# Block-causal attention feeding a max-of-two MLP on one core: a new order of the opening loads, and batch 1's transposes moved to a later step

## The chip, the core and the metric

The kernel runs on one core of a Trainium2 chip. The core has five engines that run their own instruction streams: TensorE (PE, with its weight loads as PEld), VectorE (DVE), ScalarE (ACT), GpSimd (POOL) and SyncE (SP). Each stream is executed in its own order; semaphores hold an instruction back until what it needs is there. Transfers issued by SP, ACT and POOL run on the same 16 DMA engines. The metric is the time of one execution in microseconds (us).

## What is computed

Eight batches, eight heads, 576 positions of 64 numbers; the MLP has 4608 tokens, 512 model columns and 1024 hidden ones.

```python
scores = scale * np.matmul(q, k.transpose(0, 1, 3, 2))
mask = (pos[:, None] // 64) >= (pos[None, :] // 64)
scores = np.where(mask, scores, -1e9)
attn = np.exp(scores - np.max(scores, axis=-1, keepdims=True))
attn = attn / (np.sum(attn, axis=-1, keepdims=True) + 1e-09)
attn_out = np.matmul(attn, v)                       # (8, 8, 576, 64)
x = attn_out.transpose(0, 2, 1, 3).reshape(8 * 576, 512)
g = np.maximum(x @ w1, x @ w2)
out = g @ w_out
```

## The kernel before

The attention is cut into 32 pairs of heads (`NPAIR`), four to a batch (`HP`); two pairs are a group g (16 groups, two to a batch). The loop at the end of the kernel takes one pair at each step s, 0 to 31. The streams of all engines stand in the order in which this loop writes them: nothing is reordered afterwards.

A step s has these parts. `burst_a`, called A(s) below, multiplies q and k for the first half of the score blocks into two tiles u0 and u1 of the PSUM pool `ps_s` (two buffers); ACT takes the exponential (line 258) into the tile `aT`, and POOL clears the masked corners (line 263). `burst_b`, B(s), does the rest in u2 and u3; u2 takes the buffer of u0 and u3 that of u1, so PE waits there for ACT. Between A and B stand the transposes (line 235) of one half (q or k) of the next group, T below; they need the bf16 copy of that half (`cast`, line 105, on POOL in most steps), which needs its load (`load_qk`, line 95, issued by SP into one of two raw buffers). Where `gated` is set, a tiny POOL memset into the raw buffer makes the load wait for POOL's place in the order. `copy_out` (line 242) takes the transposed q or k out of PSUM. Then `av(p, ...)` multiplies the weights of a pair by V (line 303) in two halves, avXa and avXb for pair X, and DVE normalises (lines 309, 310). `PLAN` says which pairs' av a step does: none in steps 0 and 1, pair 0 in step 2, pairs 1, 2 and 3 in step 3, none in 4 and 5, and pair s-2 from step 6 on. `x_out(g)` transposes a group's result into xT (lines 323 to 329); after the last group of a batch its 576 tokens are ready for the MLP.

The MLP is a long list of matmuls of 512 columns, called fills: units h (line 165, x by w1, then x by w2, eight matmuls to each 128 hidden columns; DVE copies the first product and takes the maximum, lines 172 and 174) and y (line 183, g by w_out; ACT copies, line 189, SP stores). `fill(n)` writes the next n of them where it stands, as far as their tokens are ready. The first 64 are the units h of the first 512 tokens, h0.0 to h0.7, and the next 32 its units y, y0.0 to y0.3. All fills, T, x_out and av take tiles of one PSUM pool, `ps_m`, with four buffers. `fill_of(s)` sets how many fills a step gets.

POOL issues the loads that change type (to bf16): V (`load_v`, line 109, five chunks c0 to c4 for a batch), w1 and w2 (`load_w`, line 120) and w_out (`load_wo`, line 123). Before the change the loads of batch 1's V stand in steps 3, 4 and 5 (`v_loads`), and those of w_out in step 5, ahead of the last chunk of V.

Of the kernel before, what the change touches and what calls it, by code (L numbers as in the profile page):

```python
# [14 lines left out]
def kernel(  # L15
# [73 lines left out]
    def load_qk(g, queues, gated=False):  # L89
        b, u = divmod(g, GPB)  # L90
        for nm, src, queue in (("q", q, queues[0]), ("k", k, queues[1])):
            raws[nm, g] = t = raw.tile([P, 2, RPP * D], FP32, name=f"{nm}raw")
            if gated:
                nc.gpsimd.memset(t[:, 0, :1], 0.0)
            queue.dma_start(
                out=t[:],
                in_=src[b, 4 * u:4 * u + 4].rearrange(
                    "(s h) (p t) d -> (h p) s (t d)", h=2, t=RPP),
            )

    def cast(nm, g, parts):
        t = raws.pop((nm, g)).rearrange("p s (t d) -> p t s d", d=D)
        qk_n[nm, g] = n = qkn.tile([P, RPP, 2, D], BF16, name=f"{nm}n")
        for copy, j0, j1 in parts:
            copy(out=n[:, j0:j1], in_=t[:, j0:j1])  # L105

    def load_v(b, c):
        rows = min(P, S - c * P)
        nc.gpsimd.dma_start(  # L109
            out=vv_r[b % NV][:rows, c, :, :D],  # L110
            in_=v[b, :, c * P:c * P + rows, :].rearrange("h p d -> p h d"),
        )
# [5 lines left out]
    def load_w(f0, fw):  # L118
        for dst, src in ((w1_sb, w1r), (w2_sb, w2r)):
            nc.gpsimd.dma_start(out=dst[:, :, f0:f0 + fw], in_=src[:, :, f0:f0 + fw])  # L120

    def load_wo(c0, n):
        nc.gpsimd.dma_start(out=wo_sb[:, c0:c0 + n, :], in_=wor[:, c0:c0 + n, :])
# [97 lines left out]
    def fill(n):  # L221
        for _ in range(min(n, ready())):
            next(moe_steps)
            at[0] += 1
# [4 lines left out]
    def transposes(nm, g, copies):  # L229
        n = qk_n.pop((nm, g))  # L230
        pts = [ps_m.tile([P, RPP, NP], BF16, name=f"ps_{nm}T", tag="m") for _ in range(2)]
        for j in range(RPP):
            for i in range(2):
                r = slice(i * NP, (i + 1) * NP)
                nc.tensor.transpose(  # L235
                    pts[i][:, j, :], n[r, j].rearrange("p s d -> p (s d)"), ident[r, r],
                )

        def copy_out():
            for i in range(2):  # L240
                t = (qT_r if nm == "q" else kT_r)[(2 * g + i) % NT]
                copies[i](  # L242
                    out=t[:, :S].rearrange("q (p j) -> q p j", j=RPP),
                    in_=pts[i].rearrange("q j p -> q p j"),
                )
        return copy_out
# [18 lines left out]
    def burst_a(p):  # L265
        u0 = ps_s.tile([P, 2, 512], FP32, name="ps_s", tag="s")
        scores(p, u0, 0, 0, 0, 512)
        u1 = ps_s.tile([P, 2, 512], FP32, name="ps_s", tag="s")
        scores(p, u1, 0, 0, 512, 64)
        scores(p, u1, 64, 1, 128, 448)  # L270
        exp(p, u0, 512, 0)
        mask(p, 0)
        exp(p, u1, 512, 512)
        mask(p, 576)

    def burst_b(p):
        u2 = ps_s.tile([P, 2, 512], FP32, name="ps_s", tag="s")
        scores(p, u2, 0, 2, 256, 320)
        scores(p, u2, 320, 3, 384, 192)
        u3 = ps_s.tile([P, 2, 512], FP32, name="ps_s", tag="s")  # L280
        scores(p, u3, 0, 4, 512, 64)
        exp(p, u2, 512, 1024)
        mask(p, 1024)
        mask(p, 1344)
        exp(p, u3, 64, 1536, m=BLK)
# [29 lines left out]
    def x_out(g):  # L315
        b, u = divmod(g, GPB)
        xp = xps.pop(g)
        pe = ps_m.tile([P, 2, NCH, BLK], BF16, name="ps_xe", tag="m")
        po = ps_m.tile([P, 2, NCH - 1, BLK], BF16, name="ps_xo", tag="m")
        for s in range(2):  # L320
            for t in range(NCH):
                src = xp[:, t, s].rearrange("p a d -> p (a d)")
                nc.tensor.transpose(pe[:, s, t, :], src[:BLK], ident[:BLK, :BLK])  # L323
                if t < NCH - 1:
                    nc.tensor.transpose(po[:, s, t, :], src[BLK:], ident[BLK:, BLK:])
        dst = xT[:, 2 * u:2 * u + 2, b * S:b * S + NCH * P].rearrange(
            "p s (t h w) -> p s t h w", h=2, w=BLK)
        nc.vector.tensor_copy(out=dst[:, :, :, 0], in_=pe[:])
        nc.vector.tensor_copy(out=dst[:, :, :NCH - 1, 1], in_=po[:])  # L329
        if u == GPB - 1:  # L330
            done_tokens[0] = (b + 1) * S
# [6 lines left out]
    def fill_of(s):  # L338
        if s >= NPAIR - LAG:
            return 27  # L340
        left = 10 - s if s < 10 else 4 - (s - 2) % 4
        return -(-ready() // left)

    def v_loads(s):
        at_ = {3: [(1, 0), (1, 1)], 4: [(1, 2), (1, 3)], 5: [(1, 4)]}
        if s in at_:
            todo = at_[s]
        else:
            nb, i = divmod(s + 2, HP)
            todo = [(nb, c) for c in ((0, 1), (2, 3), (4,), ())[i]] if s > 5 and nb < B else []  # L350
        for nb, c in todo:
            load_v(nb, c)

    cq = transposes("q", 0, (dve, act))
    ck = transposes("k", 0, (act, dve))
# [3 lines left out]
    for s in range(NPAIR):  # L359
        g, i = divmod(s, 2)  # L360
        avs = PLAN.get(s, [s - LAG])
        n = fill_of(s)
        if x_due and s > HP:
            x_out(x_due.pop())
        burst_a(s)
        if x_due and s == HP:
            x_out(x_due.pop())
            n = fill_of(s)
        if s == 0:
            cast("k", 1, ((dve, 0, RPP),))  # L370
        fill(n * 2 // 5)
        copy_out = None
        if g + 1 < NG:
            copy_out = transposes("qk"[i], g + 1, (dve, dve if s < HP else act))
            if s < HP:
                copy_out()
        burst_b(s)
        if copy_out and s >= HP:
            copy_out()
        if i == 0 and g + 2 < NG:  # L380
            load_qk(g + 2, (SP, SP), gated=s < HP)
        if g + 2 - (i == 0) < NG and s > 0:
            cast("kq"[i], g + 1 + i, ((pool, 0, RPP),))
        if s == 0:
            load_w(512, 512)
        if s == 5:
            load_wo(0, 4)
            load_wo(4, 4)
        v_loads(s)
        for p in avs:  # L390
            av(p, [0, 1])
            if s >= HP:
                fill(n // 5)
            av(p, [2, 3, 4])
            if p % 2:
                x_due.append(p // 2)
            if p == 2:
                x_out(x_due.pop())
        fill(n - n * 2 // 5 - n // 5 * (len(avs) > 0 and s >= HP))
    for p in range(NPAIR - LAG, NPAIR):  # L400
        if x_due:
            x_out(x_due.pop())
# [3 lines left out]
        fill(11)  # L406
    x_out(NG - 1)
    fill(len(needs))


# [28 lines left out]
```

## Time and profile before

| what | us |
|---|---|
| median of 3 runs | 317.12 (317.08 to 317.22) |
| the profiled execution's own time | 318.27 |
| its span in the profile | 316.5 |
| PE busy | 276.1 (87%) |
| DVE, ACT, POOL busy | 180.3, 135.9, 97.0 |
| PE idle that ended with V's load | 9.6 |
| PE idle at T that ended with a cast of q on POOL | 9.4 |

Rows of the timeline give start, duration, engine, line, operation and tiles, count, and in brackets the idle time before with what ended it. A row of several matmuls lasts until the last one's end, so the next row of the engine can start before it ends. Rows of groups end with the idle time of the engine and its releasers. Rows of waits give total, times and longest.

### The profile page before, as it was taken

To read this page: it belongs to the slowest core of one execution; us is meant where nothing else is said; L and a number is where in the kernel's file an instruction comes from. 1 tells how busy PE (TensorE), PEld (TensorE's weight loads), DVE (VectorE), ACT (ScalarE), POOL (GpSimd) and SP (SyncE) were. 2 spreads that over 40 slices of the span, in tenths; PEclk is the share of its full clock that TensorE was granted. 3 is DMA by queue.
4 is the path that set the end of the run, shared out by engine and by line. 5 is a ranking of instruction groups with operands and counts; after the bars stand their busy time and mean duration, and the time that the engine had idled before them with its cause. 6 is when DMAs were issued, how large, how long until landed. Compare 5 with 4: busy or idle time off the path is not lost.

```text
span 316.5 us, 7360 instructions
## 1 busy us (share of the span) xinstructions
PE 276.1 (87%) x3072; PEld 142.7 (45%) x3072; DVE 180.3 (57%) x361; ACT 135.9 (43%) x195; POOL 97.0 (31%) x217
## 2 busy tenths in 40 slices
PE   1517894399899999999999999999999999999995
PEld 1305542144554554455445554555454554444442
DVE  5504873163587856575667566756675675646440
ACT  3634373047755573447344734373534401010112
POOL 3934476043283263325331533153300000000000
PEclk9999999589999999999999999999999999999999
DMA  7999989908498157628672867286300000101113
GB/s 280 106 240 238 330 114 177 148 0 100 114 310 146 35 35 100 194 76 143 89 206 64 156 79 214 53 166 70 74 35 33 35 35 33 69 35 64 50 52 133
DMA packets 55649, 36.65 MB, mean 116 GB/s; under 512 B 38720, under 2 KB 42816, under 8 KB 55616
## 3 DMA queue, kind: packets, MB, share of 16 engines
q0 software_dynamic: 41728, 7.87, 30.6%
q1 hardware_dynamic: 13616, 27.73, 25.3%
q8 instruction: 24, 0.39, 0.5%
q10 hardware_dynamic: 272, 0.59, 0.5%
q14 instruction: 9, 0.07, 0.1%
HBM read 34.60 MB, written 9.44 MB: 139 GB/s over the span
## 4 chain that ended last, share of the span: by engine, by line
PE 75%; DMA 8%; POOL 6%; issue 4%; DVE 3%; ACT 3%; ACTq 0%; POOLq 0%; DVEq 0%
PE ps_h L165 37%; PE ps_y L183 19%; PE ps_o L303 9%; PE ps_s L252 6%; DMA qraw<-in_q_dram 4%; DMA vv<-in_v_dram 4%; ACT aT L258 3%; PE ps_kT L235 2%; POOL vv L109 1%; PE ps_xe L323 1%; POOL qn L105 1%; DVE kT L242 1%; DVE xp L310 1%; PE ps_qT L235 1%; POOL kn L105 1%
## 5 line engine op out<-in xcount | busy, mean ns | idle before, releaser
L165 PE MATMUL ps_h<-xT,w_sb 128*128 128x512 bf16 x576 | 138.5, 382 | 0.6 <-DVE xT L329 0.4
L258 ACT ACTIVATE aT<-ps_s 128x1024 bf16<-128x1024 f32 (+1 forms) x128 | 98.9, 833 | 90.4 <-PE ps_s L252 88.8
L165 PEld LDWEIGHTS <-w_sb 128*128 128x128 bf16 x576 | 53.4, 98 | 62.1 <-issue 6.8
L172 DVE CAST h<-ps_h 128x512 bf16<-128x512 f32 x72 | 49.6, 689 | 53.3 <-PE ps_h L165 53.3
L183 PE MATMUL ps_y<-wo_sb,g 128*128 128x512 bf16 x288 | 70.1, 379 | 0.0
L263 POOL MEMSET aT<- 64x128 bf16 x128 | 23.2, 199 | 139.3 <-ACT aT L258 138.9
L189 ACT COPY y<-ps_y 128x512 f32<-128x512 f32 x36 | 21.1, 586 | 82.1 <-PE ps_y L183 57.3
L174 DVE TENSOR_TENSOR g<-h,ps_h 128x512 bf16<-128x512 bf16 x72 | 49.4, 686 | 9.6 <-PE ps_h L165 7.9
L303 PE MATMUL ps_o<-vv,aT 128*128 128x65 bf16 x960 | 39.6, 196 | 10.6 <-DMA vv<-in_v_dram 9.6
L252 PE MATMUL ps_s<-qT,kT 64*128 64x64 bf16 (+4 forms) x384 | 37.9, 295 | 8.8 <-ACT aT L258 8.1
L303 PEld LDWEIGHTS <-aT 128*128 128x128 bf16 x960 | 34.5, 99 | 20.5 <-issue 9.9
L183 PEld LDWEIGHTS <-g 128*128 128x128 bf16 x288 | 26.6, 98 | 30.0 <-issue 1.3
L109 POOL DMA_DIRECT2D vv<-in_v_dram x40 | 33.7, 848 | 0.0
L310 DVE TENSOR_TENSOR xp<-ps_o,rec 128x256 bf16<-128x256 f32 x64 | 31.4, 491 | 2.2
L309 DVE RECIPROCAL rec<-ps_o 128x4 f32<-128x4 f32 x64 | 11.9, 186 | 33.3 <-PE ps_o L303 32.8
L252 PEld LDWEIGHTS <-kT 64*128 64x128 bf16 x384 | 18.0, 98 | 22.5 <-issue 16.6
L235 PE MATMUL ps_qT<-ident,qn 64*128 64x64 bf16 x288 | 8.1, 199 | 15.8 <-POOL qn L105 9.4
L105 POOL CAST qn<-qraw 128x1152 bf16<-128x1152 f32 (+1 forms) x16 | 18.1, 1133 | 11.2 <-DMA qraw<-in_q_dram 10.3
L242 DVE COPY qT<-ps_qT 128x576 bf16<-128x576 bf16 x18 | 13.4, 752 | 13.7 <-PE ps_qT L235 13.4
L242 DVE COPY kT<-ps_kT 128x576 bf16<-128x576 bf16 x18 | 13.4, 753 | 8.4 <-PE ps_kT L235 8.2
L105 POOL CAST kn<-kraw 128x1152 bf16<-128x1152 f32 (+1 forms) x15 | 16.6, 1103 | 0.8
L235 PEld LDWEIGHTS <-qn 64*128 64x128 bf16 x288 | 6.3, 100 | 21.2 <-POOL qn L105 10.3
(31 smaller groups left out, 84.7 us busy)
## 6 DMA issues: line engine op xcount, KB each, us to landing
qraw<-in_q_dram SPq DMA_DIRECT2D x16, 576.0 KB, 4.5
out_dram<-y SPq DMA_DIRECT2D x36, 256.0 KB, 2.0
kraw<-in_k_dram SPq DMA_DIRECT2D x15, 576.0 KB, 5.3
vv<-in_v_dram POOLq DMA_DIRECT2D x32, 128.0 KB, 4.2
w_sb<-in_moe_w_dram POOLq DMA_DIRECT2D x4, 256.0 KB, 7.5
w_sb<-in_moe_w_dram POOLq DMA_DIRECT2D x2, 512.0 KB, 12.7
wo_sb<-in_moe_w_out_dram POOLq DMA_DIRECT2D x2, 512.0 KB, 8.8
kraw<-in_k_dram ACTq DMA_DIRECT2D x1, 576.0 KB, 5.4
```

The costliest lines, as they stand in the source:

```text
L105: copy(out=n[:, j0:j1], in_=t[:, j0:j1])
L109: nc.gpsimd.dma_start(out=vv_r[b % NV][:rows, c, :, :D], in_=v[b, :, c * P:c * P + rows, :].rearrange("h p d -> p h d"),)
L165: nc.tensor.matmul(pt[:], w_sb[:, c, f * P:(f + 1) * P], xT[:, c, t0:t0 + SPAN], start=(c == 0), stop=(c == NDM - 1),)
L172: nc.vector.tensor_copy(out=h1[:], in_=pt[:])
L174: nc.vector.tensor_max(g[:, f, :], h1[:], pt[:])
L183: nc.tensor.matmul(py[:], g[:, f, s * P:(s + 1) * P], wo_sb[:, f, :], start=(f == 0), stop=(f == NFF - 1),)
L235: nc.tensor.transpose(pts[i][:, j, :], n[r, j].rearrange("p s d -> p (s d)"), ident[r, r],)
L242: copies[i](out=t[:, :S].rearrange("q (p j) -> q p j", j=RPP), in_=pts[i].rearrange("q j p -> q p j"),)
L252: nc.tensor.matmul(ps[:m, hh, col:col + w], kT[r, c * P:c * P + m], qT[r, q0:q0 + w], start=True, stop=True,)
L258: nc.scalar.activation(out=aT_r[p % NA][:m, :, a0:a0 + w], in_=ps[:m, :, :w], func=AF.Exp, scale=scale,)
L303: nc.tensor.matmul(po[:, gi, hh, :], a[:, hh, a0:a0 + P], vv[:, c, h0 + 2 * hh, :], start=(mm == 0), stop=(mm == n_mm - 1),)
L310: nc.vector.tensor_mul(xp[:, ts[0]:ts[0] + n, :, p % 2], po[:, :, :, :D], rec[:, :n].to_broadcast([P, n, 2, D]),)
```

## The change

The loads of the opening get a new order on POOL and SP, written out step by step in `pool_work`: q and k of group 3 move from step 2 to step 1 (behind the gates of group 2 in step 0); V of batch 1 moves ahead of the casts of groups 2 and 3, to steps 2, 3 and 4; w_out stands in step 5 behind all of it. The cast of q of group 2 moves from POOL in step 1 to ACT in step 3, that of k from POOL in step 2 to POOL in step 3, and the casts of group 3 from steps 3 and 4 to step 4. The loads of group 4 stay in step 4. The transposes of group 2 move out of steps 2 and 3 to the beginning of step 4, between two lots of 6 fills; those of group 3 stand together in step 5. In step 4 x_out(1) and these 12 fills come before A(4). A step's fills are dealt out otherwise: half of them (before, two fifths) between A and T in steps with more than 12, and a sixth (before, a fifth) between the two halves of av.

```diff
-    def v_loads(s):
-        at_ = {3: [(1, 0), (1, 1)], 4: [(1, 2), (1, 3)], 5: [(1, 4)]}
-        if s in at_:
-            todo = at_[s]
+    def pool_work(s):
+        g, i = divmod(s, 2)
+        if s == 0:
+            load_qk(2, (SP, SP), gated=True)
+            load_w(512, 512)
+        elif s == 1:
+            load_qk(3, (SP, SP), gated=True)
+        elif s == 2:
+            load_v(1, 0)
+            load_v(1, 1)
+        elif s == 3:
+            load_v(1, 2)
+            cast("q", 2, ((act, 0, RPP),))
+            cast("k", 2, ((pool, 0, RPP),))
+        elif s == 4:
+            load_v(1, 3)
+            load_v(1, 4)
+            cast("q", 3, ((pool, 0, RPP),))
+            cast("k", 3, ((pool, 0, RPP),))
+            load_qk(4, (SP, SP))
+        elif s == 5:
+            load_wo(0, 4)
+            load_wo(4, 4)
+            cast("q", 4, ((pool, 0, RPP),))
         else:
-            nb, i = divmod(s + 2, HP)
-            todo = [(nb, c) for c in ((0, 1), (2, 3), (4,), ())[i]] if s > 5 and nb < B else []
-        for nb, c in todo:
-            load_v(nb, c)
+            if i == 0 and g + 2 < NG:
+                load_qk(g + 2, (SP, SP))
+            if g + 1 + i < NG:
+                cast("kq"[i], g + 1 + i, ((pool, 0, RPP),))
+            nb, j = divmod(s + 2, HP)
+            if nb < B:
+                for c in ((0, 1), (2, 3), (4,), ())[j]:
+                    load_v(nb, c)
+
+    T_AT = {s: [("qk"[s % 2], s // 2 + 1)] for s in range(NPAIR - 2)}
+    T_AT[2] = T_AT[3] = T_AT[4] = []
+    T_AT[5] = [("q", 3), ("k", 3)]
+
+    def t_pair(s):
+        outs = [transposes(nm, g, (dve, dve if s < HP else act)) for nm, g in T_AT.get(s, [])]
+        return lambda: [f() for f in outs]
...
-        if x_due and s > HP:
+        if x_due:
             x_out(x_due.pop())
+        if s == HP:
+            n = fill_of(s)
+            fill(6)
+            cq = transposes("q", 2, (dve, act))
+            ck = transposes("k", 2, (dve, act))
+            cq()
+            ck()
+            fill(6)
         burst_a(s)
-        if x_due and s == HP:
-            x_out(x_due.pop())
-            n = fill_of(s)
         if s == 0:
             cast("k", 1, ((dve, 0, RPP),))
-        fill(n * 2 // 5)
-        copy_out = None
-        if g + 1 < NG:
-            copy_out = transposes("qk"[i], g + 1, (dve, dve if s < HP else act))
-            if s < HP:
-                copy_out()
-        burst_b(s)
-        if copy_out and s >= HP:
+        n_a = n // 2 if n > 12 else n * 2 // 5
+        n_b = n // 6 if avs and s >= HP else 0
+        fill(n_a)
+        if s < HP:
+            t_pair(s)()
+            burst_b(s)
+        else:
+            copy_out = t_pair(s)
+            burst_b(s)
             copy_out()
-        if i == 0 and g + 2 < NG:
-            load_qk(g + 2, (SP, SP), gated=s < HP)
-        if g + 2 - (i == 0) < NG and s > 0:
-            cast("kq"[i], g + 1 + i, ((pool, 0, RPP),))
-        if s == 0:
-            load_w(512, 512)
-        if s == 5:
-            load_wo(0, 4)
-            load_wo(4, 4)
-        v_loads(s)
+        pool_work(s)
         for p in avs:
             av(p, [0, 1])
-            if s >= HP:
-                fill(n // 5)
+            fill(n_b)
...
-        fill(n - n * 2 // 5 - n // 5 * (len(avs) > 0 and s >= HP))
+        fill(n - n_a - n_b)
```

Three places of the new order, each with the line of before marked - and that of after marked +. POOL first, in steps 1 to 3; `vv_99` is V of batch 1, `aT_102` to `aT_104` are cleared in steps 1 to 3, and the first `CAST qn` is q of group 2.

```order
 L120 DMA w_sb<-in_moe_w_dram 128x4x512 x2
 L263 MEMSET aT_102 64x2x64 x4
-L105 CAST qn<-qraw 128x1152
-L263 MEMSET aT_103 64x2x64 x4
 L94 MEMSET qraw 128x1
 L94 MEMSET kraw 128x1
+L263 MEMSET aT_103 64x2x64 x4
+L109 DMA vv_99<-in_v_dram 128x8x64 x2
+L263 MEMSET aT_104 64x2x64 x4
+L109 DMA vv_99<-in_v_dram 128x8x64
```

The cast that stood ahead of the gates of group 3 is gone from POOL, and three chunks of batch 1's V stand where group 3's casts were waited for. Next, POOL in steps 4 and 5, where the last chunks of that V and w_out are issued:

```order
+L109 DMA vv_99<-in_v_dram 128x8x64
+L109 DMA vv_99<-in_v_dram 64x8x64
 L105 CAST qn<-qraw 128x1152
-L109 DMA vv_99<-in_v_dram 128x8x64 x2
-L263 MEMSET aT_101 64x2x64 x4
 L105 CAST kn<-kraw 128x1152
-L109 DMA vv_99<-in_v_dram 128x8x64 x2
 L263 MEMSET aT_102 64x2x64 x4
+L123 DMA wo_sb<-in_moe_w_out_dram 128x4x512 x2
 L105 CAST qn<-qraw 128x1152
-L123 DMA wo_sb<-in_moe_w_out_dram 128x4x512 x2
-L109 DMA vv_99<-in_v_dram 64x8x64
```

The last chunk of V stood behind w_out and now stands ahead of it, with two casts of group 3 between. Last, PE of the changed kernel at the beginning of step 4, with the semaphores that each waits for (`ps_h_573` is the second product of h0.0, of which two matmuls are left; `DVE` and `Activation` stand for copies out of PSUM):

```order
L165 MATMUL ps_h_573<-xT_105,w2_sb_107 128x512 [waits PE_49]
...
L235 LDWEIGHTS qn_402 [waits Activation_49]
L235 MATMUL ps_qT_576<-ident_109,qn_402 128x64 [waits PE_49]
...
L235 LDWEIGHTS kn_404 [waits Pool_49]
L235 MATMUL ps_kT_596<-ident_109,kn_404 128x64 [waits DVE_49]
L235 LDWEIGHTS kn_404
L235 MATMUL ps_kT_597<-ident_109,kn_404 128x64 [waits Activation_49]
```

The transposes of k of group 2 follow those of q directly, and their second tile waits for ACT's copy of q's second tile, since the half-done product holds one of the four buffers.

## The prediction, with its working

> **What bounds the kernel now.** I read the page's slices first, then PE's groups, its waits, the chain of work and the transfers.
>
> ```profile
> PE   1517894399899999999999999999999999999995
> PEclk9999999589999999999999999999999999999999
> L303 PE MATMUL ps_o<-vv,aT 128*128 128x65 bf16 x960 | 39.6, 196 | 10.6 <-DMA vv<-in_v_dram 9.6
> L235 PE MATMUL ps_qT<-ident,qn 64*128 64x64 bf16 x288 | 8.1, 199 | 15.8 <-POOL qn L105 9.4
> ```
>
> A slice is 7.9 us. PE is full from the ninth slice on; what is missing lies in the first five and in the seventh and eighth, and in the eighth the granted clock falls to 0.5. The next rows are of the windows of a whole batch in the middle, and of PE's waits from 64 us to the end:
>
> ```profile
> 142.10:173.97 31.87, 30.75 (x372) 16.24 (x372) 20.03 (x41) 16.60 (x26) 11.50 (x25) 1.00 0.62 127
> PE ps_s L252 <- ACT aT L258: 5.5, 10, 0.7
> PE ps_o L303 <- DVE xp L310: 0.3, 2, 0.2
> ```
>
> PE is busy for 30.75 of 31.87 us there, and its waits after 64 us come to 5.8 us. So PE bounds everything behind the opening, and the time changes by what the opening moves. The chain of work shows the opening's two great waits, and the transfers issued in two short windows show their sizes (last number: us from issue to landing):
>
> ```profile
> 16.35 7.94 DMA qraw<-in_q_dram
> 24.44 1.15 POOL qn L105
> 48.37 12.16 DMA vv<-in_v_dram
> ...
> wo_sb<-in_moe_w_out_dram POOLq DMA_DIRECT2D x1, 512.0 KB, 10.3
> vv<-in_v_dram POOLq DMA_DIRECT2D x1, 64.0 KB, 12.2
> ...
> w_sb<-in_moe_w_dram POOLq DMA_DIRECT2D x2, 512.0 KB, 12.7
> kraw<-in_k_dram SPq DMA_DIRECT2D x1, 576.0 KB, 10.4
> ```
>
> First, T of q of group 2 stands in step 2 and waits for a load that lands at 24.3. Second, av4 in step 6 waits for the last 64 KB of batch 1's V, which were issued behind w_out and took 12.2 us.
>
> **The change part by part.** No matmul, cast, copy or byte is added or removed, so the steps are placed again on PE's line with these rows of the timeline:
>
> ```profile
> 13.29 1.04 PE L252 MATMUL ps_s<-qT,kT 64*128 64x512 bf16 x6 [1.06 <-ACT aT L258]
> 15.93 0.23 PE L252 MATMUL ps_s<-qT,kT 64*128 64x64 bf16 x2 [0.30 <-ACT aT L258]
> 16.84 1.04 PE L252 MATMUL ps_s<-qT,kT 64*128 64x512 bf16 x6 [0.68 <-ACT aT L258]
> 25.64 0.66 PE L235 MATMUL ps_qT<-ident,qn 64*128 64x64 bf16 x18 [7.76 <-POOL qn L105]
> 26.71 1.83 PE L303 MATMUL ps_o<-vv,aT 128*128 128x65 bf16 x30
> 31.25 2.00 PE L303 MATMUL ps_o<-vv,aT 128*128 128x65 bf16 x60
> 31.73 0.17 DVE L309 RECIPROCAL rec<-ps_o 128x4 f32<-128x4 f32 x1
> 37.29 0.41 DVE L329 COPY xT<-ps_xo 128x512 bf16<-128x512 bf16 x1
> 37.76 1.02 PE L165 MATMUL ps_h<-xT,w_sb 128*128 128x512 bf16 x4 [0.38 <-DVE xT L329]
> 38.99 0.41 PE L252 MATMUL ps_s<-qT,kT 64*128 64x320 bf16 x6
> 39.34 2.33 PE L165 MATMUL ps_h<-xT,w_sb 128*128 128x512 bf16 x10
> 40.57 0.63 ACT L242 COPY qT<-ps_qT 128x576 bf16<-128x576 bf16 x1
> 40.58 0.35 POOL L263 MEMSET aT<- 64x128 bf16 x2 [2.57 <-ACT aT L258]
> 40.99 1.14 POOL L105 CAST kn<-kraw 128x1152 bf16<-128x1152 f32 x1
> 41.60 0.61 PE L252 MATMUL ps_s<-qT,kT 64*128 64x512 bf16 x6
> 42.07 1.75 POOL L109 DMA_DIRECT2D vv<-in_v_dram  x2
> 43.54 0.44 PE L235 MATMUL ps_kT<-ident,kn 64*128 64x64 bf16 x18
> 46.90 1.49 POOL L123 DMA_DIRECT2D wo_sb<-in_moe_w_out_dram  x2
> 60.87 3.18 PE L165 MATMUL ps_h<-xT,w_sb 128*128 128x512 bf16 x7
> 68.27 0.91 PE L303 MATMUL ps_o<-vv,aT 128*128 128x65 bf16 x24 [0.18 <-DVE xp L310]
> 71.45 0.82 PE L183 MATMUL ps_y<-wo_sb,g 128*128 128x512 bf16 x3
> ```
>
> Unit prices: ten fills take 2.33 us with the last one's 0.38 of latency, so one takes 0.217. From their starts to the next row's, A takes 0.54, T 0.27 and B 0.41; avXa takes 0.19 and avXb 0.74, which is 0.91 less the last one's 0.2.
>
> *Steps 2 and 3.* Without T, these run as step 1 did, held by ACT: A(1) to A(2) is 3.55, and A(1) to u3's matmuls 2.64. From A(2) at 16.84, u3 of step 2 starts at 19.48 and ends at 19.7. av0 takes 1.83, to 21.5; its V was loaded in the opening and did not hold it before. A(3) follows at 21.5, and u3 ends at 24.4. av1 so starts at 24.4 instead of 31.25: 6.85 earlier.
>
> *av1 to the first full fill.* Before, this took 6.5 (31.25 to 37.76). DVE is busy nearly throughout (31.73 to 37.70), so it stays 6.5. PE was slow after its long idle time: 30 matmuls took 1.83 at 26.71, and 60 took 2.00 at 31.25. How much of av1 to av3 now runs slowly the trace does not show: between nothing and one av, 0.9. I take 0.5, near the middle, since PE has then had 5 us of broken work, against 5.6 us of nearly unbroken work by 31.25. The fill starts at 31.4. The Trainium skill (TensorE: Matmul & The Clock Gate, "What's actually happening") puts the warm-up at one window of about 3.4 us of activity; by it av1 would start warm and the sum be 0.5 better, and the rows fit either.
>
> *Step 4.* Four fills to 32.3; T of q ends 0.44 later, at 32.7. T of k waits for ACT's copy, a new wait: 0.63 and two hand-offs of some 0.15, to 33.6. Then T 0.27, six fills 1.3, A(4) 0.54, eight fills 1.73, B 0.41 and eight fills 1.73: A(5) at 39.6. ACT's cast of q of group 2 comes after step 3's exponentials, about 25.2 to 26.5 if it costs about what POOL's does (1.14), with q landed at 24.3; POOL's cast of k starts at 27.2 (16.83 and 10.4) and ends at 28.4. Both are over 4 us early, which is their cover.
>
> *Step 5.* POOL clears step 4's corners 1.6 after B(4) starts (38.99 to 40.58 before), so about 39.1, issues two chunks of V (1.6 to 1.75) and casts q and k of group 3 until 42.2 and 43.3. PE does A(5) and seven fills by 41.7 and waits for both casts: 1.1 of new waiting. T of k ends at 43.6, B at 44.0, seven fills at 45.5. The second halves of w1 and w2, needed from about 40.8, landed at about 30 before (12.7 after an issue near 17); group 3's loads now overlap with them, at most some 5 us more (priced under the first rival).
>
> *Steps 6 and 7.* POOL issues w_out (1.49) from 45.5 and casts q of group 4 until 48.1. PE reaches T at 47.6 and waits 0.5. B to 48.8, av4a and two fills to 49.5, av4b to 50.2, five fills to 51.3. The last chunk of V is issued by 41; at the 5.4 us that the chunks before it took (quoted below) it lands at 46.4, about 3 us early, so the stall of 9.6 goes, and with it the slow clock behind it, seven fills in 3.18 instead of 1.5. Step 7: A, seven fills, T, B, av5a and one fill, 3.15: the first y at 54.5.
>
> ```profile
> vv<-in_v_dram POOLq DMA_DIRECT2D x2, 128.0 KB, 5.4
> 53.70:71.45 17.75, 10.71 (x114) 4.76 (x113) 6.77 (x14) 3.69 (x6) 3.49 (x7) 0.71 0.59 81
> ```
>
> *Sum.* Before, the first y stood at 71.45, with av5b, x_out(2) and A(8) already done; these are 1.6 of PE's time, so the like point is at 56.1, 15.3 earlier. The rows of before have hand-offs beside my prices: ten fills from 39.34 end at 41.51 and A starts at 41.60; A and six fills from there end at 43.44 and T starts at 43.54. That is about 0.2 a step, 0.8 for four. w_out's second half, issued at 46.3 with its old 10.3, lands at 56.6, and the fifth matmul of y needs it at 56.1: 0.5. I take 14.0. Through step 9 both kernels have done 96 fills, so the like point carries to the end; the other dealing of the fills I cost at nothing, since PE has work on either side.
>
> The sum is against 318.27 (span 316.5 and 1.77 around it), which gives 304.3; the median is 1.15 below that execution, so 317.12 - 14.0 = **303.1**. About 0.2% is what a measurement of this kernel can tell from no change.
>
> **The rivals.**
>
> *The loads collide.* For: the load of group 3 now starts near 18.8 instead of 28.4, beside group 2's and the weights, and the core's transfers moved 243 GB/s (last number) when these were all under way:
>
> ```profile
> 24.00:32.00 8.00, 5.94 (x108) 4.39 (x109) 4.26 (x10) 4.05 (x6) 3.54 (x10) 1.00 1.07 243
> ```
>
> Group 3's two loads of 576 KB are 4.9 us at that rate. Were k of group 2 late by that and by two chunks of V (some 2.6), its cast would end at 35.9 instead of 28.4, T of k would stand 2.3 later, and w_out some 2 to 3 later too. Price 2 to 6: 305 to 309. Against: SP's queue has q and k of group 2 in front, and the second part of every load has 3 us or more of slack. The Trainium skill (DMA: Bandwidth & Descriptors, "Issuing engines are not separate DMA queues") says that transfers of all issuing engines interleave on the same 16 DMA engines, which speaks for it; no row of before shows SP's loads of two groups beside the weights.
>
> *The other dealing costs.* With one fill less between the halves of av, avXb comes 0.217 sooner after avXa and may wait for DVE to free a buffer. There are 17 such steps behind step 10: 3.7 at most, to 306.8. Against: PE's waits for anything but ACT are 0.3 after 64 us.
>
> *PE stays slow, and the kernel ends slower.* PE now has short waits in steps 2 to 6 and may never get its full clock before y. For: at 60.87 seven fills took 3.18, about 0.43 each, in a window with a mean granted clock of 0.71. 64 fills cost 0.21 more each, 13.4; three av 0.9 each, 2.7; A (1.04 for 0.61) and T (0.66 for 0.44) 2.6 in four steps: 18.7 in all, so 4.7 slower than before, 321.8. It decides against the change if slowness lasts over about three quarters of the way from 24 to 54 us. Against: from 37 to 49 before, between waits of 0.4 us and less, fills run at 0.217; my longest new wait is 1.1. The Trainium skill (same page on TensorE, "A second HAM failure mode: psum-queue depth-cycling") reports clocks that oscillate when PE idles briefly and often, which is this rival; this trace shows none after 64 us.
>
> *It does nothing.* V's place in the stall would have to be taken by w_out: y would need it to land at 70, against 57. I see no way.
>
> **How the numbers follow.** Forecast 0.69 (gain 11.5 to 15.8, so 301.3 to 305.6), collision 0.16, dealing 0.09, slow PE 0.05, nothing 0.01. Faster 0.94, same 0.01, slower 0.05. The range runs from 301.3, all covers holding and no hand-offs, to 308.5, which takes in most of the collision and all of the dealing; it leaves out about 0.15.
>
> **What would show it.** Right: PE's wait for V is gone, and so is the row of T at 25.64; av1 starts near 24.4, the first full fill near 31.4, A(5) near 39.6, the first y near 54.5; PE waits about 1 us for POOL's casts in step 5; the granted clock does not fall to 0.5. Wrong: a wait for DMA of over 2 us on V, w_out or group 2, fills at 0.43, or a middle batch longer than 31.87.

## The result, and the profile after

| | before | after |
|---|---|---|
| median of the runs of one chip | 317.17 us (317.08 to 318.92, 4 runs) | 304.69 us (304.46 to 305.11, 4 runs) |
| the profiled execution's own time | 318.27 | 304.71 |
| its span | 316.5 | 302.9 |
| PE busy | 276.1 (87%) | 276.1 (91%) |

The ratio is 0.9595, with a 95% interval of 0.9561 to 0.963. The kernel is 12.5 us faster by the medians and 13.56 by the two profiled executions; PE does the same work and idles less. The slices and groups of the page of after that answer to those of before:

```profile
PE   1577889998998999999998999899999999999994
PEclk9999999999999999999999999999999999999999
L303 PE MATMUL ps_o<-vv,aT 128*128 128x65 bf16 x960 | 40.5, 198 | 0.9 <-ACT y L189 0.5
L235 PE MATMUL ps_qT<-ident,qn 64*128 64x64 bf16 x288 | 7.8, 196 | 8.3 <-DVE qn L105 6.4
```

A slice is now 7.6 us. The hole in the fourth slice and that in the seventh and eighth are gone, and so is the fall of the granted clock. In the row of av 0.9 us of idle time are left of 10.6, none of it for a load; in that of T 8.3 of 15.8, and 6.4 of these are the kernel's first wait, for q of group 0, which both kernels have. PE's waits in the first 72 us (total, times, longest) name what came in their place:

```profile
PE ps_qT L235 <- POOL qn L105: 1.9, 2, 1.6
PE ps_kT L235 <- POOL kn L105: 0.7, 1, 0.7
PE ps_kT L235 <- ACT qT L242: 0.6, 1, 0.6
```

Of the first row 1.6 is T of group 1 in step 0, as before. The rest, 0.3, 0.7 and 0.6, are new waits of steps 4 and 5. They stand in brackets in PE's timeline of after, which has the landmarks of the prediction:

```profile
19.52 0.24 PE L252 MATMUL ps_s<-qT,kT 64*128 64x64 bf16 x2 [0.30 <-ACT aT L258]
24.27 3.15 PE L303 MATMUL ps_o<-vv,aT 128*128 128x65 bf16 x60
31.58 1.02 PE L165 MATMUL ps_h<-xT,w_sb 128*128 128x512 bf16 x4 [0.37 <-DVE xT L329]
33.78 0.42 PE L235 MATMUL ps_kT<-ident,kn 64*128 64x64 bf16 x17 [0.64 <-ACT qT L242]
40.10 0.61 PE L252 MATMUL ps_s<-qT,kT 64*128 64x512 bf16 x6
42.59 0.44 PE L235 MATMUL ps_qT<-ident,qn 64*128 64x64 bf16 x18 [0.27 <-POOL qn L105]
43.69 0.61 PE L235 MATMUL ps_kT<-ident,kn 64*128 64x64 bf16 x18 [0.66 <-POOL kn L105]
45.13 1.46 PE L165 MATMUL ps_h<-xT,w_sb 128*128 128x512 bf16 x6 [0.27 <-DVE kT L242]
55.38 0.38 PE L183 MATMUL ps_y<-wo_sb,g 128*128 128x512 bf16 x1
```

The last chunks of batch 1's V, issued from 39.8 us on, and w_out behind them (last number: us from issue to landing):

```profile
vv<-in_v_dram POOLq DMA_DIRECT2D x1, 64.0 KB, 4.0
wo_sb<-in_moe_w_out_dram POOLq DMA_DIRECT2D x2, 512.0 KB, 8.2
```

The 64 KB that took 12.2 us behind w_out take 4.0 ahead of it. A batch in the middle, from the first whole av of step 18 to that of step 22:

```profile
129.33:161.34 32.01, 30.90 (x375) 16.14 (x373) 20.15 (x40) 16.71 (x25) 11.54 (x26) 1.00 0.61 127
```

This is 0.14 longer than before (31.87), and PE is busy for 0.15 more of it.

### The profile page after: what moved, and what is told of

Read it like the earlier page. It is cut to its first block, busy times and chain, and to the rows that moved or that the text cites. A ratio compares the mean times of both kernels' runs of the same rounds, so it can differ in the third digit from the quotient of the medians.

```text
span 302.9 us, 7360 instructions
## 1 busy us (share of the span) xinstructions
PE 276.1 (91%) x3072; PEld 143.0 (47%) x3072; DVE 179.8 (59%) x359; ACT 138.4 (46%) x198; POOL 96.0 (32%) x216
## 4 chain that ended last, share of the span: by engine, by line
PE 82%; ACT 6%; DVE 3%; issue 3%; POOL 3%; DMA 2%; ACTq 0%
PE ps_h L165 40%; PE ps_y L183 20%; PE ps_o L303 11%; PE ps_s L252 7%; ACT aT L258 6%; PE ps_kT L235 2%; DMA qraw<-in_q_dram 2%; PE ps_xe L323 2%; POOL vv L109 1%; PE ps_qT L235 1%; DVE xp L310 1%; POOL qn L105 1%; DVE kT L242 1%; POOL kn L105 1%; ACT y L189 1%
## 5 line engine op out<-in xcount | busy, mean ns | idle before, releaser
L165 PE MATMUL ps_h<-xT,w_sb 128*128 128x512 bf16 x576 | 136.7, 379 | 0.9 <-DVE xT L329 0.4
L165 PEld LDWEIGHTS <-w_sb 128*128 128x128 bf16 x576 | 52.7, 98 | 61.3 <-issue 5.6
L183 PE MATMUL ps_y<-wo_sb,g 128*128 128x512 bf16 x288 | 69.4, 379 | 0.1
L252 PE MATMUL ps_s<-qT,kT 64*128 64x64 bf16 (+4 forms) x384 | 37.5, 292 | 10.6 <-ACT aT L258 9.9
L303 PE MATMUL ps_o<-vv,aT 128*128 128x65 bf16 x960 | 40.5, 198 | 0.9 <-ACT y L189 0.5
L303 PEld LDWEIGHTS <-aT 128*128 128x128 bf16 x960 | 35.5, 100 | 11.0 <-DVE xp L310 4.7
L310 DVE TENSOR_TENSOR xp<-ps_o,rec 128x256 bf16<-128x256 f32 x64 | 31.4, 491 | 2.2
L309 DVE RECIPROCAL rec<-ps_o 128x4 f32<-128x4 f32 x64 | 11.9, 186 | 27.5 <-PE ps_o L303 26.9
L242 DVE COPY kT<-ps_kT 128x576 bf16<-128x576 bf16 x17 | 12.7, 754 | 11.5 <-PE ps_kT L235 11.5
L105 POOL CAST qn<-qraw 128x1152 bf16<-128x1152 f32 (+1 forms) x15 | 17.0, 1134 | 5.3 <-DMA qraw<-in_q_dram 4.5
L242 DVE COPY qT<-ps_qT 128x576 bf16<-128x576 bf16 x17 | 12.7, 752 | 4.3 <-PE ps_qT L235 4.1
L242 ACT COPY qT<-ps_qT 128x576 bf16<-128x576 bf16 x15 | 9.5, 632 | 7.1 <-PE ps_qT L235 7.1
## 6 DMA issues: line engine op xcount, KB each, us to landing
w_sb<-in_moe_w_dram POOLq DMA_DIRECT2D x2, 512.0 KB, 16.3
```

The lines of the kernel that those rows point to most:

```text
L165: nc.tensor.matmul(pt[:], w_sb[:, c, f * P:(f + 1) * P], xT[:, c, t0:t0 + SPAN], start=(c == 0), stop=(c == NDM - 1),)
L183: nc.tensor.matmul(py[:], g[:, f, s * P:(s + 1) * P], wo_sb[:, f, :], start=(f == 0), stop=(f == NFF - 1),)
L242: copies[i](out=t[:, :S].rearrange("q (p j) -> q p j", j=RPP), in_=pts[i].rearrange("q j p -> q p j"),)
L252: nc.tensor.matmul(ps[:m, hh, col:col + w], kT[r, c * P:c * P + m], qT[r, q0:q0 + w], start=True, stop=True,)
L303: nc.tensor.matmul(po[:, gi, hh, :], a[:, hh, a0:a0 + P], vv[:, c, h0 + 2 * hh, :], start=(mm == 0), stop=(mm == n_mm - 1),)
L310: nc.vector.tensor_mul(xp[:, ts[0]:ts[0] + n, :, p % 2], po[:, :, :, :D], rec[:, :n].to_broadcast([P, n, 2, D]),)
```

## The experiments

All times are medians in us (range, number of runs) with the ratio to the kernel before, measured beside them, and its 95% interval. The medians of before were 317.55 beside e1 to e4, 318.32 beside e5 to e8, 317.6 beside e9 and e10, and 318.75 beside e11 and e12.

| run | median | ratio |
|---|---|---|
| after | 304.69 (304.46 to 305.11, 4) | 0.9595 [0.9561, 0.963] |
| e1_v_ahead | 307.65 (307.24 to 307.86, 4) | 0.9679 [0.9651, 0.9706] |
| e2_wo_ahead | 314.01 (313.5 to 314.82, 6) | 0.9885 [0.986, 0.9909] |
| e3_old_deal | 304.60 (304.34 to 304.78, 4) | 0.9584 [0.9557, 0.9611] |
| e4_before_again | 318.01 (316.79 to 320.36, 12) | 1.0011 [0.9987, 1.0035] |
| e5_t2_first | 303.57 (302.7 to 305.57, 6) | 0.9546 [0.9516, 0.9576] |
| e6_t3_split | 303.18 (303.11 to 303.95, 5) | 0.9537 [0.9512, 0.9561] |
| e7_t2_t3 | 302.48 (302.26 to 302.91, 5) | 0.9511 [0.9487, 0.9534] |
| e8_warm | 304.31 (303.08 to 304.97, 6) | 0.9565 [0.9536, 0.9594] |
| e9_all | 303.80 (303.26 to 304.82, 6) | 0.9579 [0.9547, 0.961] |
| e10_q4 | 303.97 (302.65 to 304.41, 5) | 0.9567 [0.9536, 0.9598] |
| e11_cast_behind | 301.19 (300.52 to 301.67, 4) | 0.9453 [0.9426, 0.948] |
| e12_cast_behind_warm | 301.42 (300.29 to 302.01, 5) | 0.9449 [0.9418, 0.948] |

### e1_v_ahead: one part alone

Before, with only the place of the last chunk of batch 1's V changed:

```diff
+        v_loads(s)
         if s == 5:
             load_wo(0, 4)
             load_wo(4, 4)
-        v_loads(s)
```

> The kernel before with one edit: in step 5 the last chunk of batch 1's V is issued ahead of w_out. Theory (two waits, each with its own price): the chunk lands at about 51.3 instead of 60.5, PE waits for it some 0.5 us instead of 9.6 and the clock does not fall, so the gain is 9.1 + 1.6 = 10.7 us: about 306.4. That is most of the whole change's 12.5, and what moving the transposes and the other loads adds is about 2 us, though av1 starts 7 us earlier with it. Rival (the loads bound the opening, one only passes its place to the next): w_out and the later loads come late in its place, PE waits for them before y, gain under 6 us: over 311. Rival (the earlier transposes carry the gain): gain under 4 us.

It gave 307.65: this one line is 9.9 of the gain. PE's timeline of e1 shows that the load still comes late, by 1.26 where 0.5 was expected, and that the first great wait is still there:

```profile
25.10 0.66 PE L235 MATMUL ps_qT<-ident,qn 64*128 64x64 bf16 x18 [7.50 <-POOL qn L105]
51.68 0.34 PE L303 MATMUL ps_o<-vv,aT 128*128 128x65 bf16 x6 [1.26 <-DMA vv<-in_v_dram]
```

### e2_wo_ahead: the other parts alone

After, with the last two chunks of V behind w_out (in the kernel before, only the last one stood there):

```diff
         elif s == 4:
-            load_v(1, 3)
-            load_v(1, 4)
...
             load_wo(0, 4)
             load_wo(4, 4)
+            load_v(1, 3)
+            load_v(1, 4)
```

> The changed kernel with one edit back: the last two chunks of batch 1's V are issued in step 5 behind w_out. Theory (POOL's transfers are served in the order of issue): they land at 57.5 to 59, PE waits 7 to 9 us for them at av4b in step 6 and is slow for some 3 us behind it: 304.7 + 8.5 to 10.5 = 313 to 315. Rival (the transfers share the engines evenly, so 192 KB come through beside 1 MB): a wait of 2 to 4 us, 307 to 309.

It gave 314.01, in the expected range, so all other parts together gain some 3.5, and with e1's 9.9 this makes the whole. The wait itself was shorter than expected: PE waited 4.92 and 0.53 for the two chunks, not 7 to 9. It came to them later, since T of q of group 4 waited 1.57 for a cast that stands on POOL behind the four issues. PE's timeline of e2, and the transfers that POOL issued in step 5:

```profile
56.85 0.66 PE L303 MATMUL ps_o<-vv,aT 128*128 128x65 bf16 x9 [4.92 <-DMA vv<-in_v_dram]
58.33 2.32 PE L165 MATMUL ps_h<-xT,w_sb 128*128 128x512 bf16 x5
```

```profile
wo_sb<-in_moe_w_out_dram POOLq DMA_DIRECT2D x2, 512.0 KB, 7.1
vv<-in_v_dram POOLq DMA_DIRECT2D x1, 128.0 KB, 9.4
vv<-in_v_dram POOLq DMA_DIRECT2D x1, 64.0 KB, 9.7
```

The small chunks of V, issued behind the two large loads, take 9.4 and 9.7; in after, ahead of them, the last one takes 4.0. The five fills behind the wait run at 0.46 us each: the slow clock follows the wait here too.

### e3_old_deal: the other dealing of fills

```diff
-        n_a = n // 2 if n > 12 else n * 2 // 5
-        n_b = n // 6 if avs and s >= HP else 0
+        n_a = n * 2 // 5
+        n_b = n // 5 if avs and s >= HP else 0
```

> The changed kernel with the former dealing of the fills (two fifths between A and T, a fifth between the halves of av). Theory (the new dealing costs about 0.14 us a batch, since a batch in the middle takes 32.00 us from av to av against 31.86 before): the batch is back at 31.86, and the time 0.5 to 0.7 us lower, 304.1. Rival (the dealing is free and the 0.14 comes from elsewhere): 304.7, the batch still 32.00.

It gave 304.60, no difference from after that can be told. The trace says why; the rows of the whole av in steps 14 and 18, of after and then of e3:

```profile
97.33 1.08 PE L303 MATMUL ps_o<-vv,aT 128*128 128x65 bf16 x30
129.33 1.08 PE L303 MATMUL ps_o<-vv,aT 128*128 128x65 bf16 x30
```

```profile
97.66 1.08 PE L303 MATMUL ps_o<-vv,aT 128*128 128x65 bf16 x30
129.52 1.08 PE L303 MATMUL ps_o<-vv,aT 128*128 128x65 bf16 x30
```

The former dealing takes 31.86 a batch against 32.00, but it is 0.33 behind at step 14: it is the worse one in the opening and the better one after it. e9 to e12 use each where it is better.

### e4_before_again: the kernel before once more

No edit. It was to tell whether the profiled execution of before, 1.15 us above its median, is long because of its wait for V.

> The kernel before, unchanged, with a second profile. Theory (its first profiled execution was a long one, 318.27 against a median of 317.12, because its wait for batch 1's V was long): a profiled execution at the median shows a wait of about 8.5 us there instead of 9.6, and all else alike. Rival (the 1.15 us lie outside the span or in many places): a wait of 9.6 again, whatever the time.

The median was 318.01, and the profiled execution took 317.81 with this wait for V (total, times, longest):

```profile
PE ps_o L303 <- DMA vv<-in_v_dram: 9.9, 1, 9.9
```

So the wait is as long, and the time is not above the median. That theory fell. Before simply scatters more than its three runs showed (316.79 to 320.36 here), while after and e3 scatter by 0.65 and less. Why it does stays open. Its twelve executions have almost the same mean granted clock over their span (0.984 in ten of them, which alone cover the whole range), so the clock does not explain it. The spread of 2.9 in e5 does go with the clock: its one long execution (305.57) is the only one of six with a mean granted clock of 0.994, and the other five, at 1.000, lie between 302.7 and 303.88.

### e5_t2_first: T of group 2 ahead of all fills of step 4

```diff
-            fill(6)
             cq = transposes("q", 2, (dve, act))
             ck = transposes("k", 2, (dve, act))
             cq()
             ck()
-            fill(6)
+            fill(12)
```

> The changed kernel with one edit: in step 4 the transposes of group 2 stand ahead of all 12 fills, in the time in which PE waits for xT. Theory (the new wait for ACT's copy, 0.64 us, and the 0.37 us wait for xT are both paid because no buffer of PSUM is free and nothing stands in between): A(4) starts 1.0 us earlier, at 34.5, and the lead carries to the end: 303.7. Rival (the step is held by DVE or by the casts of step 5, not by PE): A(4) earlier, but the lead is lost at the casts of group 3 in step 5, which wait for POOL, 304.5 or more.

It gave 303.57, 1.1 less than after: T of k and its copies now run while DVE still makes xT, and PE's wait of 0.64 for ACT's copy is gone. A(4) starts at 34.48 instead of 35.54, and the lead of 1.07 is still there at step 14 (0.17 of it stands at av1 already, ahead of the edit):

```profile
34.48 0.61 PE L252 MATMUL ps_s<-qT,kT 64*128 64x512 bf16 x6
```

### e6_t3_split: T of group 3 in two steps

```diff
             cast("k", 2, ((pool, 0, RPP),))
+            cast("q", 3, ((act, 0, RPP),))
+            cast("k", 3, ((pool, 0, RPP),))
         elif s == 4:
             load_v(1, 3)
             load_v(1, 4)
-            cast("q", 3, ((pool, 0, RPP),))
-            cast("k", 3, ((pool, 0, RPP),))
...
-    T_AT[2] = T_AT[3] = T_AT[4] = []
-    T_AT[5] = [("q", 3), ("k", 3)]
+    T_AT[2] = T_AT[3] = []
```

> The changed kernel with group 3's casts in step 3 (q on ACT, k on POOL) and its transposes as everywhere else, q in step 4 and k in step 5. Theory (step 5 pays 0.27 + 0.66 + 0.27 us for casts that stand behind two issues of V on POOL): these three waits go, 1.2 us, and w_out is issued about 1 us earlier: 303.5. Rival (loads): q and k of group 5 then load some 10 us earlier, beside V of batch 1, whose last chunks come late, and PE waits for them at av4b: 305 or more.

It gave 303.18, 1.5 less than after. The three waits of step 5 (0.27, 0.66 and 0.27) are gone, A(6) starts at 44.55 instead of 46.52 (0.27 of this lead stands at av1 already), and T of group 4 now waits for its cast, by 0.42:

```profile
44.55 0.61 PE L252 MATMUL ps_s<-qT,kT 64*128 64x512 bf16 x6
47.20 0.44 PE L235 MATMUL ps_qT<-ident,qn 64*128 64x64 bf16 x18 [0.42 <-POOL qn L105]
```

### e7_t2_t3: e5 and e6 together

> Both edits together, the group 2 transposes ahead of the fills and the group 3 casts in step 3. Theory: the two leads add up, 2.2 us, to 302.5, with no wait of PE for a transfer after 31 us. Rival (w_out comes to bound it): y is reached 2.2 us earlier and w_out's second half, which lands just in time now (56.2 against 56.7), is not early enough: PE waits 1 to 2 us at the fifth matmul of y, 303.5 to 304.5.

It gave 302.48, as expected: the two gains add to 2.2 of 2.6, and PE does not wait for w_out.

### e8_warm: what the slow clock costs between av0 and av3

After, with 26 transposes of the identity in each of steps 2 and 3, into a tile that nobody reads, where PE waits for ACT:

```diff
+    def warm_up(n):
+        pt = ps_m.tile([P, RPP, NP], BF16, name="ps_w", tag="m")
+        for j in range(n):
+            nc.tensor.transpose(pt[:, j % RPP, :], ident[:NP, :], ident[:NP, :NP])
...
     def burst_b(p):
+        if p in (2, 3):
+            warm_up(18)
...
+        if p in (2, 3):
+            warm_up(8)
```

> The changed kernel with 26 transposes of the identity more in each of steps 2 and 3, in PE's waits for ACT, into a tile that nobody reads. Theory (the clock is low at av1 because PE was not busy enough before, and this costs what av1 to the first full fill took more than the 6.5 us of before, 0.8 us): the 60 matmuls of av1 and av2 take 2.0 us instead of 3.15, and the time falls by 0.5 to 0.8, to about 304.0. Rival (DVE's chain holds this stretch whatever the clock): the matmuls are quick, the time stays within 0.2 of 304.7. Second rival (the clock needs more than PE's share): they still take 3.15.

The row of av1 and av2 in e8 (its line 312 is line 303 of after):

```profile
24.19 2.00 PE L312 MATMUL ps_o<-vv,aT 128*128 128x65 bf16 x60
```

It is 2.00 instead of 3.15; the first full fill starts at 30.70 and A(5) at 39.22, both 0.88 earlier. So the clock cost after 0.8 to 0.9 in this stretch. The medians (304.31 and 304.69) show less of it, because e8's six executions are of two kinds. Three have a mean granted clock of 0.998 to 1.000 and take 303.08 to 303.88, which is about 0.8 less than after (304.46 to 305.11, all at 1.000). The other three have 0.993 or 0.994 and take 304.73 to 304.97: there the clock falls for a time (3.4 us at half of it make 0.994), and the gain is lost. At which place it falls in those three was not traced.

### e9_all and e10_q4: two misses

e9 is e7 with the warming of e8 and, from step 10 on, the former dealing of fills. e10 also casts q of group 4 one step sooner:

```diff
             load_v(1, 3)
             load_v(1, 4)
             load_qk(4, (SP, SP))
+            cast("q", 4, ((pool, 0, RPP),))
         elif s == 5:
             load_wo(0, 4)
             load_wo(4, 4)
-            cast("q", 4, ((pool, 0, RPP),))
```

> The changed kernel with four edits together: the group 2 transposes ahead of the fills, the group 3 casts in step 3, the transposes of the identity in PE's waits of steps 2 and 3, and the former dealing of the fills from step 10 on. Theory (each is a wait of its own on PE's line, so they add up): 302.5 for the first two, 0.9 less with a clock that is up at av1 to av3 (it stayed low up to 29.7 in the profile of the first two), 0.6 less for the dealing, 0.14 a batch: 301.0. Rival (the 0.14 a batch is given back in the opening, as the kernel with the former dealing everywhere came out only 0.1 lower): 301.6 or more.

> The same with q of group 4 cast in step 4, ahead of w_out's issue, where POOL has nothing else. Theory: the wait of 0.42 us at the transposes of step 6 goes, 0.3 to 0.4 us lower than the kernel with the four edits: 300.6. Rival (w_out bounds y by now): PE waits that time at y instead, no difference.

They gave 303.80 and 303.97, some 3 us more than expected and more than e7. ACT's and PE's timelines of e9, and its windows of 4 us (behind the window stand its length and PE's busy time; the granted clock is the third number from the end):

```profile
30.44 1.15 ACT L105 CAST qn<-qraw 128x1152 bf16<-128x1152 f32 x1 [4.36 <-DMA qraw<-in_q_dram]
31.50 0.63 ACT L242 COPY qT<-ps_qT 128x576 bf16<-128x576 bf16 x1
```

```profile
32.18 0.40 PE L165 MATMUL ps_h<-xT,w_sb 128*128 128x512 bf16 x1 [1.08 <-ACT qT L242]
32.80 3.81 PE L165 MATMUL ps_h<-xT,w_sb 128*128 128x512 bf16 x10 [0.22 <-issue]
36.55 0.61 PE L252 MATMUL ps_s<-qT,kT 64*128 64x512 bf16 x6
```

```profile
28.00:32.00 4.00, 1.81 (x64) 1.36 (x61) 3.40 (x9) 1.56 (x2) 0.07 (x1) 1.00 1.12 289
32.00:36.00 4.00, 3.60 (x9) 1.37 (x10) 1.09 (x2) 0.67 (x2) 1.15 (x1) 0.57 1.18 322
```

ACT's cast of q of group 3 waits for its load. ACT's copy of qT of group 2 stands behind it, so it starts at 31.50, and PE waits 1.08 for the buffer. (In e7 the copy stands behind the same cast and starts at 31.34, but PE comes to it later and does not wait.) Then ten fills take 3.81 where ten took 2.33 before, in a window with a mean granted clock of 0.57. The warmed kernel comes sooner to the place where it has to wait. Two theories were left: the cast in front of the copy, or the warming and the half-idle stretch behind it.

### e11_cast_behind and e12_cast_behind_warm: the two theories apart

e11 is e10 without the warming and with ACT's cast written behind its copies; e12 is e11 with the warming.

```diff
             cast("k", 2, ((pool, 0, RPP),))
-            cast("q", 3, ((act, 0, RPP),))
             cast("k", 3, ((pool, 0, RPP),))
...
             cq()
             ck()
+            cast("q", 3, ((act, 0, RPP),))
             fill(12)
```

> The edits of e10 without the added identity transposes of steps 2 and 3, and with ACT's cast of group 3's q moved to behind ACT's copies of q2 and k2 in step 4, so that its wait for the load (until 31.5 us in e9) holds no copy of ACT. Theory (in e9 and e10 the wait of the cast held ACT's copy of qT, PE idled 1.0 us at it and then took its ten fills at 0.38 us each): the wait of 1.08 us for ACT's copy goes, no stretch of fills after 32 us stands over 0.30 us a fill, and the time is that of T of group 2 and of group 3 together less the 0.4 of the wait at T of group 4 and about 0.5 of the former dealing from step 10 on: 301.5 (300.9 to 302.2). Rival (the slow fills come of the half-busy stretch at 28 to 32 us, whatever ACT does): fills after 32 us at 0.35 or more, 302.5 to 304. Second rival: the cast behind the copies is late for T in step 4, a wait of 0.5 or more there, 302 to 303.

> e11 with 26 identity transposes into a tile that nobody reads in each of steps 2 and 3, as in e8. Theory: as e11, and av1 and av2 take 2.0 us instead of 3.15 to 3.5, worth 0 to 0.9 where the fills behind are not slow: 301.0 (300.4 to 301.7). Rival (the clock falls again at 32 us because PE comes to the work of step 4 sooner and waits there for its data): fills after 32 us at 0.35 us or more, 302.5 to 304, that is slower than e11.

e11 gave 301.19, the fastest kernel of the study by its median, 3.5 below after (by the ratios to before 0.9453 against 0.9595). e12 gave 301.42, which cannot be told from it, though its av1 and av2 take 2.00 instead of 3.48. Against e7, e11 leads by 0.76 at step 14 (94.59 and 95.35): 0.29 of it stands at A(4) already, and 0.42 is the wait at T of group 4. From there the former dealing adds 0.14 a batch (0.90 at step 18). ACT's timeline of e11, then PE's rows of step 4 of e11 and of e12:

```profile
31.05 0.64 ACT L242 COPY qT<-ps_qT 128x576 bf16<-128x576 bf16 x1 [5.25 <-PE ps_qT L235]
32.05 0.64 ACT L242 COPY kT<-ps_kT 128x576 bf16<-128x576 bf16 x1 [0.37 <-PE ps_kT L235]
32.59 1.15 ACT L105 CAST qn<-qraw 128x1152 bf16<-128x1152 f32 x1
```

```profile
31.24 0.75 PE L235 MATMUL ps_kT<-ident,kn 64*128 64x64 bf16 x18 [0.32 <-DVE xT L328]
31.92 2.76 PE L165 MATMUL ps_h<-xT,w_sb 128*128 128x512 bf16 x11
34.62 0.61 PE L252 MATMUL ps_s<-qT,kT 64*128 64x512 bf16 x6
```

```profile
30.57 0.96 PE L235 MATMUL ps_kT<-ident,kn 64*128 64x64 bf16 x18
32.30 2.58 PE L165 MATMUL ps_h<-xT,w_sb 128*128 128x512 bf16 x10 [0.22 <-issue]
34.81 0.61 PE L252 MATMUL ps_s<-qT,kT 64*128 64x512 bf16 x6
```

In both, the wait of 1.08 is gone, so that wait was the cast's. In the profiled execution of e12 the clock still falls, this time at 29.4 us already, and A(4) starts 0.19 later than in e11 although av1 and av2 ended 1.2 sooner. So the theory holds for the wait, and its rival for the clock, though the fall comes sooner than the rival said.

The fall comes with the warming. Of the 22 executions of the four warmed kernels (e8, e9, e10, e12), 17 have a mean granted clock of 0.994 or less; of the 28 of after, e3, e5, e6, e7 and e11, one has. It does not come every time: two of e12's five executions have 1.000, and they take 300.29 and 300.35, less than any of e11 (300.52 to 301.67), while the other three take 301.42 to 302.01. So warming gains where the clock stays up afterwards, and loses it again where the clock falls; by the medians it pays nothing here. e9's miss is the wait and the fall together.

## Why the prediction was right, and where its sizes were off

The mechanism held: both great waits went, nothing waits for V or w_out, and PE takes the rest at nearly its old pace. One of the prediction's own signs of being wrong did come, though by little: a middle batch longer than 31.87 (32.01). The steps one by one:

| step | predicted | found |
|---|---|---|
| u3's matmuls of step 2 | 19.48 | 19.52 |
| av1 starts | 24.4 | 24.27 |
| first full fill | 31.4 | 31.58 |
| A(5) | 39.6 | 40.10 |
| new waits of step 5 | 1.1 | 1.2 (0.27, 0.66, 0.27) |
| wait at T of q of group 4 | 0.5 | none |
| first y | 54.5 | 55.38 |
| like point, from 71.45 | 56.1, then 0.8 and 0.5 off | 57.37 |
| gain at the end, profiled execution | 14.0 | 13.56 |

- *av1 to the first full fill* took 7.3 where the prediction has 6.5 and 0.5 for the slow clock. e8 puts the clock at 0.8 to 0.9, near the upper bound of one av. The Trainium skill (TensorE: Matmul & The Clock Gate, "What's actually happening"), by which av1 would have started warm and 0.5 been won, is not borne out for work as broken as this: after more than 7 us of it, 60 matmuls still took 3.15. (The page's table says of this activity that it is sustained.)
- *Step 4*: the new wait of T of k for ACT's copy was forecast and came (0.64). e5 shows that it was worth removing.
- *Step 5*: the two casts held PE by 0.93, and a third wait, 0.27 of a fill for DVE's copy of kT, was not foreseen.
- *Hand-offs*: the sum took 0.8 off for what its steps leave out, and the first y came 0.88 later than those steps say. The like point is worked out as A(8)'s end, 58.67, less six more matmuls of y that after has done by then (1.3): 57.37, 14.08 before that of the kernel before.
- *w_out*: the half of a microsecond for it was not needed; its second half landed at about 56.2, and the fifth y, the fourth matmul behind 56.67, starts at about 57.3. That the sum agrees at the like point (14.08 against 14.0) is in part luck: this term and the missing wait at T of group 4 stood against the two that were too small.
- *The other dealing of fills*, costed at nothing, is the first term mis-sized: 0.14 a batch, so that the lead shrinks from 14.12 at step 14 to 13.55 at the last 32 matmuls of y. Over the whole kernel it costs next to nothing (e3), since it gains in the opening what it loses behind; but the steps of the prediction were laid out with the new dealing, and only the loss was left out. Its cause was not the wait that the rival named: PE waits no longer than before, and is busy for 0.15 more. What this busy time is was not settled.
- *From the profiled execution to the median* is the second: "the median is 1.15 below that execution, so 317.12 - 14.0". After's profiled execution is at its median (304.71 and 304.69), so the offset should not have been carried over; that is 1.15 of the miss of 1.6 between 303.1 and 304.69, and the dealing is most of the rest. e4 shows that the offset is no property of the execution that was profiled. Of 12 runs of before the median was 318.01, so 317.12 was a low draw of three.

The 6.85 by which av1 comes sooner are not what this part gains in the end. e1 still has the first great wait, and after is only 3.0 faster than e1 (2.5 by the profiled executions); 1.26 of that is e1's remaining wait for V. What stands against the 6.85 is shown by the experiments that take it away: T of k's wait 1.1 (e5), step 5's waits 1.5 (e6), 2.2 for the two together (e7), the slow clock 0.8 (e8). A(4) adds 0.54: in the kernel before it ran at 35.32, while PE would have waited for DVE, and now it follows the fills. This makes 3.5, and with the 1.2 to 1.7 that are left of the gain 4.7 to 5.2. The rest, 1.6 to 2.1, was not traced.

Of the rivals, the collision of loads cost PE nothing: group 2's k landed at 27.5 (27.2 was forecast). Loads beside it took longer (the second halves of w1 and w2 a median of 16.3 us instead of 12.7), but within their slack, and no wait for a load stands in PE's rows of after beyond those that both kernels have. The slow clock did not last. The clock does fall in other kernels, as e2, e9 and e12 show, but there too it came back, after 3.4 us in e9 and e12 and 6.8 in e2.

## What to carry to other kernels

A small load that is needed soon belongs ahead of a large one that is needed late: on POOL's queue the same 64 KB took 4.0 us ahead of w_out and 9.7 to 12.2 behind it, and one line moved was some four fifths of this gain. The same holds for an engine's own stream: a cast that waits for a load belongs behind the copies that others wait for. A wait removed is worth what the next waits leave of it, so price the next ones, and read the offset between a profiled execution and a median of three as scatter until more runs say otherwise.

## What the runs showed of the hardware

How broken PE's work may be before its clock stays low: in the window from 20 to 24 us PE was busy for 3.00 to 3.10 of 4 us in the six kernels without warming (after, e3, e5, e6, e7, e11), and av1 and av2 took 3.15 to 3.48; with 3.32 to 3.70 in the four warmed ones they took 2.00. If the busy share decides, the limit lies between; no run varied the share alone. These are the rows of after and of e8:

```profile
20.00:24.00 4.00, 3.10 (x38) 1.96 (x36) 1.36 (x4) 2.42 (x5) 2.25 (x5) 1.00 1.20 290
```

```profile
20.00:24.00 4.00, 3.37 (x64) 2.71 (x62) 1.36 (x4) 2.47 (x5) 2.25 (x5) 1.00 1.19 296
```

Both give a granted clock of 1.00, so the durations tell of a slow start here, and the clock's column does not. That the clock falls in e12 at 29.4 us with no wait over 0.46 us from 24 us on was not expected either. Its windows of 1 us, and then the same three of e8:

```profile
26.00:27.00 1.00, 0.80 (x31) 0.65 (x27) 0.93 (x5) 0.10 (x1) 0.15 (x1) 1.00 1.12 294
28.00:29.00 1.00, 0.56 (x15) 0.32 (x11) 0.93 (x5) 0.00 (x0) 0.90 (x1) 1.00 1.06 273
30.00:31.00 1.00, 0.77 (x22) 0.56 (x18) 0.97 (x3) 0.40 (x1) 0.00 (x0) 0.50 1.12 295
```

```profile
26.00:27.00 1.00, 0.80 (x31) 0.65 (x27) 0.93 (x5) 0.10 (x1) 0.15 (x1) 1.00 1.13 298
28.00:29.00 1.00, 0.56 (x15) 0.31 (x11) 0.93 (x5) 0.00 (x0) 0.46 (x1) 1.00 1.13 290
30.00:31.00 1.00, 0.62 (x4) 0.22 (x3) 0.65 (x2) 0.00 (x0) 0.00 (x0) 1.00 1.15 299
```

Up to 29 us PE's share is the same in both (0.80 to 0.56), yet the clock fell in e12 and not in e8. The granted clock was low for 3.41 us in e9, e10 and e12 alike, for 6.83 in e2 and for 10.24 in the kernel before (from windows of 0.05 us): once, twice and three times the same length. The Trainium skill (same page and section) says that the activity is taken in windows of about 3.4 us that run free of the kernel. The lengths agree with that figure. Windows that run free would let the same work fall in one execution and not in another, as in e8 and e12; that they do is shown by no run here, and the cause stays open.
